# Fill matmuls at the start, Q casts straight from PSUM and a new instruction order in a chunk-select attention + ELU MLP kernel

## The chip, the cores and the metric

The kernel runs on one core of a Trainium2 chip. The metric is the device time of one execution in microseconds; the time before is 295.12 us, the median of three runs (294.37 to 295.87). The profiled execution has a span of 295.9 us.

A core has five engines with in-order queues of their own: TensorE (PE, matmuls and weight loads), VectorE (DVE), ScalarE (ACT), GpSimd (POOL) and SyncE (SP, which here only issues DMA transfers). Matmul results go to PSUM[...]; everything else is in SBUF.

## The reference, cut to what matters

Attention over 4 batches x 8 heads, 768 positions, head size 64. Per query, an upper bound of the score of each chunk of 32 keys selects the 6 best causal chunks; softmax attention runs over these. Then an MLP with 512 inputs, 2048 hidden units and ELU:

```python
k_min, k_max = k_chunks.min(axis=3), k_chunks.max(axis=3)        # per chunk of 32 keys
ub = sum(maximum(q * k_min, q * k_max), axis=-1)                 # per query and chunk
top_chunks = argsort(where(causal, ub, -1e9))[..., -6:]
scores = where(selected and causal, q @ k.T / 8, -1e9)
x = softmax(scores) @ v                                          # -> (3072, 512)
h = x @ w_in
out = where(h > 0, h, exp(minimum(h, 0)) - 1) @ w_out
```

## The kernel before, in words

The sequence of each batch is cut into blocks of queries: batch 0 into three of 256, the others into two of 384 (`CUTS`), nine blocks in all. Heads are taken in four pairs j, so a pair's K or Q is 128 partitions wide (two heads of 64).

For a block i, `load` brings K, Q and V in fp32, one DMA for each 128 positions. `prep_k(j, i)` transposes a pair's K on PE with the fp32 identity into a PSUM tile (L484), DVE takes maximum and minimum per chunk from it (L504) and forms their difference (L521), and ACT casts K to bf16: for the blocks in `DIRECT_K` (0 and 1) in one instruction per head straight from PSUM into `lhs` (L511), for others through `kb` and a DMA (L516, L519). `prep_q(j, i)` transposes Q in the same manner, ACT copies it to SBUF as `QTf` in fp32 (L534), and a bf16 cast per head goes into `rhs`: on ACT from `QTf` for the blocks in `QC_ACT` (0 and 1, L538), on POOL for the others (L542). DVE makes `Qrl`, the positive part (L545). The PSUM tile of K and Q is a `psM` bank for block 0 (`PSM_PREP`), of which there are four, and the single `psT` bank for every other block.

`select(i)` computes the bounds of all pairs with small fp32 matmuls (L563), DVE transposes them (L574), takes the eight largest per query (L581), compares (L585) and transposes the mask into rows 64 to 95 of `rhs` (L591 for blocks 0 to 2; for others L597 and a DMA `rhs<-msk`). `attend` computes scores (L625) with the mask as additional contraction rows, ACT takes the exponential (L641, L645), DVE multiplies the diagonal parts by a triangle (L652, L659), PE weighs V (L674), DVE divides (L683, L685), and the result is transposed into `xt` (by PE and DVE, L693 and L696, for the first and last block; by DMA, L698, for the others). `mlp` runs 16 hidden tiles (L713; ACT exponential L717, POOL minus one L719, DVE maximum and minimum L721) and then the output product (L732, ACT copy L736, store).

At the start DVE also initialises: `rhs` and `kst` and `selb` memsets (L774, L777, L779), the constant `econst` (L405) and the mask rows of four `lhs` tiles (L418).

The order is not written by hand. `Plan` takes every operation with an engine, a cost (`occ`), a latency (`lat`) and a priority, and lays them out in time: each engine takes the operation that can start first, and among those that can start at once the one with the lowest priority number. The operation list in this order is then emitted, so the plan fixes each engine's queue; on the chip each instruction still waits for its own semaphores. A priority is that of the stage (`span`) plus a number from `SHIFTS` for the stage, the engine and the block. `CAPS` is how many buffers of a kind exist.

Before each PE operation planned before `FILL_END` (70 us), the emission loop puts fill matmuls on a junk tile (L849) into planned holes, and a run of them ahead of the first real PE operation, whose number comes from that operation's planned start:

```python
for _ in range(int((o.start - pe - 100) / FILL_NS) if pe else int((o.start - FILL_FROM) / 90)):
    nc.tensor.matmul(o_bank[:, 400:512], lhsT=junk, rhs=junk[:, 0:112], start=True, stop=True)
```

The POOL queue issues the weights and some K, Q and V loads in the fixed order `SW_ORDER`, the first of them after a gate operation that reads the first K tile.

## Time and profile before

| | before |
|---|---|
| time, median of 3 | 295.12 us |
| span of the profiled execution | 295.9 us |
| PE busy | 277.3 us (94%), 2544 matmuls, 100 of them fills |
| DVE busy | 204.8 us (69%) |
| ACT busy | 196.4 us (66%) |
| POOL busy | 137.0 us (46%) |
| mean granted TensorE clock | 0.965 |
| DMA | 36.23 MB, mean 122 GB/s |

In a row of the profile, L-numbers are lines of the kernel; `out<-in` gives the tiles with their numbers left out; a bracket `[0.61 <-PE psM L484]` is the engine's idle time before the instruction and what ended it. PE's busy time covers matmuls from start to a modelled end, overlapping ones once, so a PE that is always busy need not be at its best rate. The clock is given as a share of full speed. A DMA share of 1.0 or more means that the core's 16 DMA engines have work all the time.

### The profile page before, as it was taken

How to read it: one execution, taken by the hardware profiler on the slowest of the kernel's cores; microseconds unless marked ns; L12 is line 12 of the kernel's file. 1: busy time of each engine (PE TensorE's matmuls, PEld its weight loads, DVE VectorE, ACT ScalarE, POOL GpSimd, SP SyncE). 2: the span in 40 equal slices, each digit the busy share in tenths (PEclk: the TensorE clock that was granted, in tenths of full speed). 3: DMA queues.
4: the chain of work that ended last, by engine and by line, in shares of the span. 5: the costliest groups of instructions: out<-in, count | busy, mean ns of one | idle time of the engine just before them, and what ended most of it. 6: DMA issues, size and time to landing. Idle time of an engine off the chain costs nothing.

```text
span 295.9 us, 7293 instructions
## 1 busy us (share of the span) xinstructions
PE 277.3 (94%) x2544; PEld 179.4 (61%) x2544; DVE 204.8 (69%) x667; ACT 196.4 (66%) x458; POOL 137.0 (46%) x278
## 2 busy tenths in 40 slices
PE   8576879999999998999999999999999999999993
PEld 8354557569658655666565556766565456655541
DVE  8778698897768886855699966666678727634620
ACT  2795587299559528997397349995496389854621
POOL 7697674034915924845365414750285024404510
PEclk9865798999999999999999999999999999999999
DMA  8889998268936665968845662602210420010001
GB/s 189 221 149 214 273 198 149 65 174 180 208 66 180 150 135 122 243 158 205 199 95 153 144 175 68 153 16 85 74 44 17 82 94 2 0 39 35 38 35 72
DMA packets 86885, 36.23 MB, mean 122 GB/s; under 512 B 74176, under 2 KB 82880, under 8 KB 86848
## 3 DMA queue, kind: packets, MB, share of 16 engines
q1 hardware_dynamic: 79424, 27.38, 37.7%
q0 software_dynamic: 5344, 7.87, 13.0%
q10 hardware_dynamic: 2080, 0.52, 0.8%
q8 instruction: 20, 0.33, 0.5%
q14 instruction: 17, 0.14, 0.2%
HBM read 27.26 MB, written 6.29 MB: 113 GB/s over the span
## 4 chain that ended last, share of the span: by engine, by line
PE 73%; DVE 13%; ACT 6%; DMA 4%; issue 2%; POOL 1%; SPq 0%; POOLq 0%; DVEq 0%; ACTq 0%
PE psM L713 23%; PE psM L732 23%; PE psS L625 10%; PE o_bank L674 6%; PE psT L484 5%; DVE gT L721 3%; PE psT L563 2%; DMA rhs<-msk 2%; PE o_bank L849 2%; ACT rhs L538 2%; DVE rhs L591 2%; DVE kmx L504 2%; ACT lhs L511 1%; DMA kld<-in_k_dram 1%; DVE thr L581 1%
## 5 line engine op out<-in xcount | busy, mean ns | idle before, releaser
L719 POOL TENSOR_SCALAR e<-e 128x384 f32<-128x384 f32 (+1 forms) x144 | 69.8, 489 | 120.6 <-ACT e L717 60.0
L713 PE MATMUL psM<-xt,w_in_sb 128*128 128x384 bf16 (+1 forms) x576 | 109.0, 313 | 1.6 <-DVE gT L721 1.4
L732 PE MATMUL psM<-w_out_sb,gT 128*128 128x512 bf16 x384 | 99.1, 379 | 0.0
L641 ACT ACTIVATE pt<-psS 128x384 bf16<-128x384 f32 (+1 forms) x164 | 87.7, 568 | 13.2 <-PE psS L625 12.7
L721 DVE SCALAR_TENSOR_TENSOR gT<-psM,e 128x384 bf16<-128x384 f32 (+1 forms) x144 | 71.8, 506 | 25.4 <-POOL e L719 24.0
L717 ACT ACTIVATE e<-psM 128x384 f32<-128x384 f32 (+1 forms) x144 | 68.8, 486 | 21.9 <-PE psM L713 18.4
L713 PEld LDWEIGHTS <-w_in_sb 128*128 128x128 bf16 x576 | 55.4, 99 | 28.1 <-issue 2.4
L625 PE MATMUL psS<-rhs,lhs 96*128 96x384 bf16 (+2 forms) x304 | 66.3, 286 | 2.5 <-DMA rhs<-msk 1.5
L732 PEld LDWEIGHTS <-gT 128*128 128x128 bf16 x384 | 36.0, 98 | 31.5 <-issue 1.2
L625 PEld LDWEIGHTS <-lhs 96*128 96x128 bf16 x312 | 29.4, 100 | 19.4 <-issue 2.3
L542 POOL TENSOR_SCALAR rhs<-QTf 64x384 bf16<-64x384 f32 (+1 forms) x56 | 29.4, 526 | 14.4 <-ACT QTf L534 10.8
L736 ACT ACTIVATE osb<-psM 128x512 f32<-128x512 f32 x24 | 14.4, 600 | 30.5 <-PE psM L732 30.3
L674 PEld LDWEIGHTS <-pt 128*128 128x128 bf16 x672 | 27.8, 99 | 9.8 <-issue 1.7
L674 PE MATMUL o_bank<-vext,pt 128*128 128x65 bf16 x672 | 30.9, 195 | 0.8 <-DVE on L685 0.5
L652 DVE TENSOR_TENSOR pt<-pt,tri 128x512 bf16<-128x512 bf16 x36 | 17.0, 475 | 7.0 <-ACT pt L641 6.6
L516 ACT ACTIVATE kb<-psT 128x384 bf16<-128x384 f32 (+1 forms) x28 | 13.7, 489 | 12.0 <-DVE kst L504 7.8
L504 DVE TENSOR_REDUCE kmx<-psT 128x12 f32<-128x384 f32 (+1 forms) x32 | 16.6, 519 | 6.7 <-PE psT L484 6.3
L534 ACT ACTIVATE QTf<-psT 128x384 f32<-128x384 f32 (+1 forms) x32 | 15.9, 498 | 7.6 <-PE psT L484 7.6
L475 POOL TENSOR_SCALAR vext<-vld 128x384 bf16<-128x384 f32 (+1 forms) x36 | 17.5, 509 | 5.7 <-DMA vld<-in_v_dram 3.0
L685 DVE TENSOR_TENSOR on<-o_bank,rcp 128x384 bf16<-128x384 f32 (+1 forms) x36 | 18.2, 506 | 0.6
L484 PE MATMUL psT<-ident_f,kld 128*128 128x128 f32 x88 | 16.0, 285 | 1.3 <-ACT QTf L534 0.6
L484 PE MATMUL psT<-ident_f,qld 128*128 128x128 f32 x88 | 15.8, 285 | 1.4 <-ACT lhs L511 1.0
(69 smaller groups left out, 241.6 us busy)
## 6 DMA issues: line engine op xcount, KB each, us to landing
out_dram<-osb SPq DMA_DIRECT2D x24, 256.0 KB, 2.2
kld<-in_k_dram SPq DMA_DIRECT2D x19, 256.0 KB, 4.0
qld<-in_q_dram SPq DMA_DIRECT2D x19, 256.0 KB, 3.9
vld<-in_v_dram SPq DMA_DIRECT2D x18, 256.0 KB, 3.5
lhs<-kb SPq DMA_DIRECT2D x48, 48.0 KB, 2.6
w_in_sb<-in_moe_w_in_dram POOLq DMA_DIRECT2D x4, 512.0 KB, 9.5
w_out_sb<-in_moe_w_out_dram POOLq DMA_DIRECT2D x4, 512.0 KB, 11.9
vld<-in_v_dram POOLq DMA_DIRECT2D x6, 256.0 KB, 5.0
```

Of the source, the lines that this page charges most:

```text
L484: nc.tensor.transpose(ps.get()[:, P * n:P * (n + 1)], xb.get()[:, n, hs, :].rearrange("p h d -> p (h d)"), ident_f)
L504: nc.vector.tensor_reduce(out=out, in_=psk.get()[:, 0:w].rearrange("p (c w) -> p c w", w=CHUNK), axis=AX.X, op=o)
L542: pool_op(110 + pool_ns(w), lambda h=h: nc.gpsimd.tensor_scalar(out=rhs[RH[i]][0:64, h, j, 0:w], in0=qtf.get()[64 * h:64 * h + 64, 0:w], s ...
L625: nc.tensor.matmul(sps.get()[:, o + pc:o + pc + n], lhsT=lhs[s][0:96, hd, P * kb:P * (kb + 1)], rhs=rhs[y][0:96, hd, j, c0 - lo:c0 - lo + ...
L641: op("ACT", act_ns(wtot), 140, lambda pt=pt, sps=sps, hd=hd, wtot=wtot: nc.scalar.activation(out=pt.get()[:, hd, 0:wtot], in_=sps.get()[:, ...
L674: nc.tensor.matmul(o3.get()[:, hd, qi, :], lhsT=pt.get()[:, hd, P * qt + off:P * qt + off + P], rhs=vexts[s][:, kb, hd, :], start=(kb == 0 ...
L685: op("DVE", dve_ns(w), 140, lambda: nc.vector.tensor_tensor(out=on.get()[:, 0:nt, :, :].rearrange("p q h d -> p h q d"), in0=o3.get()[:, : ...
L713: op("PE", 1 + w / 2.4, 200, lambda fc=fc, kk=kk, h_ps=h_ps: nc.tensor.matmul(h_ps.get()[:, 0:w], lhsT=w_in_sb[:, kk, P * fc:P * (fc + 1)] ...
L717: op("ACT", act_ns(w), 200, lambda e=e, h_ps=h_ps: nc.scalar.activation(out=e.get()[:, 0:w], in_=h_ps.get()[:, 0:w], func=AF.Exp), reads=[ ...
L719: op("POOL", pool_ns(w), 72, lambda e=e: nc.gpsimd.tensor_scalar(out=e.get()[:, 0:w], in0=e.get()[:, 0:w], scalar1=-1.0, scalar2=1.0, op0= ...
L721: g_ops.append(op("DVE", dve_ns(w), 130, lambda e=e, h_ps=h_ps, fc=fc: nc.vector.scalar_tensor_tensor(out=gT[fc // 4].get()[:, fc % 4, 0:w ...
L732: op("PE", 216, 200, lambda tt=tt, fc=fc, o_ps=o_ps: nc.tensor.matmul(o_ps.get(), lhsT=gT[fc // 4].get()[:, fc % 4, P * tt:P * (tt + 1)], ...
```

## The change

It has four parts.

1. The run of fill matmuls ahead of the first real PE operation is a fixed 30 (`FILL_FIRST`) in place of a number worked out from the plan. It was 79 in the kernel before.
2. For blocks 0 and 1 the two Q casts per pair read the PSUM tile itself and no longer the fp32 copy `QTf`; `QTf` is still made, for the bounds.
3. The planner assumes shorter latencies for what happens in the first 30 us (`EARLY`): 800 instead of 1500 ns after a DMA's last byte, and a margin of 20 instead of 80 ns after an engine operation. The cost of issuing a DMA from SP is taken as 20 to 30 ns more. Where an operation needs two buffers of one kind, it now waits until two are free.
4. All `SHIFTS` are new, found by a search over orders with that planner, so the order of all queues may differ.

The rest (spaces, an unused `VC_ACT`, a DVE form of the Q cast that no block uses) changes nothing that is emitted. The core of the diff:

```diff
-QC_ACT = (0, 1)
-VC_ACT = ()
+QC = {0: "ACT", 1: "ACT"}
...
+EARLY = 30e3
 FILL_NS = 500
-FILL_FROM = 1500
+FILL_FIRST = 30
 FILL_END = 70e3
 SHIFTS = {
...
-    ('init', 'DVE'): (2.32119, 0.0, 0.0, 4.74909, 8.35134, 25.74829, 26.2034, 24.17884, 8.09583),
+    ('init', 'DVE'): (0.44568, 0.0, 0.0, 7.20875, 0.34149, 0.36288, -7.77657, 2.31749, 2.55692),
...
-    ('prep_k', 'ACT'): (-19.18919, -30.78931, -27.5262, -6.91647, -6.7488, -6.36581, -3.55271, -15.77301, -8.33444),
-    ('prep_k', 'DVE'): (-28.28537, -41.41256, -18.41797, -26.42048, 4.76573, -40.62348, -18.36229, -14.34176, -9.12351),
+    ('prep_k', 'ACT'): (1.95557, 3.69513, -7.38461, -10.46153, -0.26086, -4.37445, -1.8812, -6.64019, -13.4638),
+    ('prep_k', 'DVE'): (13.79969, 29.17587, 8.56117, 5.61227, 22.14159, 14.74266, 22.42925, 17.17039, 5.0524),
...
-    ('prep_q', 'ACT'): (-33.9716, -32.60888, -11.98557, -31.52365, -6.14348, -38.53006, -19.34522, -0.18424, -32.21482),
+    ('prep_q', 'ACT'): (-7.71405, -9.34431, -9.87241, -11.61367, -10.7821, -10.84415, -1.41335, -1.46186, -6.15349),
...
-    ('score', 'ACT'): (-15.06279, 15.94173, -8.66685, 9.77749, -9.24225, 2.15661, -0.32595, 11.29037, -1.82453),
+    ('score', 'ACT'): (8.71172, 10.04522, 4.64753, 3.02921, -4.28376, 5.74632, 0.24677, -9.22653, 3.34877),
...
+                    need = {}
                     for x in o.bufs:
                         if x not in held:
-                            t = max(t, min(slots[x.cls], default=1e18))
+                            k = need[x.cls] = need.get(x.cls, 0) + 1
+                            t = max(t, sorted(slots[x.cls])[k - 1] if len(slots[x.cls]) >= k else 1e18)
...
-                done.end = clock + DMA_END
+                done.end = clock + (800 if clock < EARLY else DMA_END)
...
-                o.end = t + o.occ + o.lat + MARGIN
+                o.end = t + o.occ + o.lat + (20 if t < EARLY else MARGIN)
...
         for h in range(2):
-            if i in QC_ACT:
-                op("ACT", 150 + act_ns(w), 60, lambda h=h: nc.scalar.activation(
-                    out=rhs[RH[i]][0:64, h, j, 0:w], in_=qtf.get()[64 * h:64 * h + 64, 0:w], func=AF.Copy),
-                    reads=[qtf], writes=[r_q[RH[i]][j]])
+            how, r_out = QC.get(i, "POOL"), [r_q[RH[i]][j]]
+            if how == "ACT":
+                op("ACT", 60 + act_ns(w), 90, lambda h=h: nc.scalar.activation(
+                    out=rhs[RH[i]][0:64, h, j, 0:w], in_=psq.get()[64 * h:64 * h + 64, 0:w], func=AF.Copy),
+                    reads=[psq], writes=r_out)
                 continue
...
-                    for _ in range(int((o.start - pe - 100) / FILL_NS) if pe else int((o.start - FILL_FROM) / 90)):
+                    for _ in range(int((o.start - pe - 100) / FILL_NS) if pe else FILL_FIRST):
```

## The prediction

> **What bounds the kernel now.** I read four views in this order: the slices of the page, the busy time by stage, the chain at its end for the price of a matmul, and the timeline of the first 25 us. The slices come first because they show where TensorE (PE) is short of work and of clock.
>
> ```profile
> PE   8576879999999998999999999999999999999993
> PEclk9865798999999999999999999999999999999999
> DMA  8889998268936665968845662602210420010001
> ```
>
> A slice is 7.4 us. From the eighth slice on PE is full and at full clock; before that it has holes, the clock falls to 0.5, and the transfers are the busiest thing. The same by stage (span, then busy us and instructions of PE, weight loads, DVE, ACT, POOL; clock; DMA share; GB/s):
>
> ```profile
> 0.00:7.30 7.30, 6.20 (x78) 6.21 (x79) 5.98 (x15) 1.49 (x2) 5.12 (x23) 1.00 0.81 189
> 7.30:60.00 52.70, 42.54 (x412) 29.45 (x410) 42.09 (x165) 34.85 (x92) 31.07 (x56) 0.81 0.90 181
> 60.00:200.00 140.00, 137.16 (x1319) 91.24 (x1318) 105.50 (x337) 103.94 (x246) 71.95 (x144) 1.00 0.61 148
> 200.00:281.00 81.00, 80.99 (x697) 47.99 (x695) 49.69 (x150) 53.80 (x116) 27.81 (x54) 1.00 0.16 47
> 281.00:295.90 14.90, 10.42 (x49) 4.51 (x46) 1.59 (x3) 2.28 (x4) 1.02 (x2) 1.00 0.14 53
> ```
>
> Busy PE is not useful PE: the 78 matmuls of the first stage are fills. So I price the useful work by its dense spacing. The chain's end gives two prices, 4.55/28 = 162.5 ns for a 384-column matmul and 10.37/48 = 216 ns for a 512-column one:
>
> ```profile
> 276.51 4.55 PE psM L713 x28
> 281.06 10.37 PE psM L732 x48
> ```
>
> From other dense runs of the trace: 256 columns of L713 109 ns, L674 30 ns, an fp32 transpose (L484) 108.5 ns, scores (L625) 58, 112 and 165 ns for 128, 256 and 384 columns, a select group (L563) 0.4, 0.81, 1.03 or 1.45 us for 64, 192, 256 or 384 queries. The sum: L713 384 x 162.5 + 192 x 109 = 83.3 us; L732 384 x 216 = 82.9; L625 37.4; L674 672 x 30 = 20.2; L484 192 x 108.5 = 20.8; L563 9.2; L693 1.1; in all 255 us. By start times 30.0 of it lie before 60 us, 134.3 in 60 to 200, 80.5 in 200 to 281, 10.1 after. So PE time lost is 30.0, 5.7, 0.5 and 4.8 us. PE is the bound, and a change that leaves its work alone can gain only from the first 30 us of loss (7.3 before any real matmul, 22.7 from there to 60) and from the 5.7.
>
> The start, from the timeline and the transfer list:
>
> ```profile
> 1.10 6.44 PE L849 MATMUL o_bank<-junk 128*128 128x112 bf16 x79 [1.10 <-DVE junk L767]
> 4.26 2.93 DVE L418 COPY lhs<-econst 32x1536 bf16<-32x1536 bf16 x4
> 7.37 1.05 PE L484 MATMUL psM<-ident_f,kld 128*128 128x128 f32 x8
> 7.81 0.76 DVE L504 TENSOR_REDUCE kmx<-psM 128x8 f32<-128x256 f32 x2 [0.61 <-PE psM L484]
> 8.99 1.37 ACT L511 ACTIVATE lhs<-psM 64x256 bf16<-64x256 f32 x4 [6.68 <-DVE kst L504]
> kld<-in_k_dram ACTq DMA_DIRECT2D x1, 256.0 KB, 4.1
> ```
>
> The second half of block 0's K, issued at 0.98, landed 4.1 us later, at 5.1 (the SP half at 4.6). The transposes started at 7.37, right behind the fills: 2.3 us of an in-order queue stood between data and work. But DVE, whose reductions come next, was itself busy with L418 until 7.19; only 0.61 us of it was a wait for PE.
>
> **What the Trainium skill says.** "TensorE: Matmul & The Clock Gate", Part 1, has a cold clock of half rate that a window of some 3.4 us of activity releases. The trace agrees: fills start 93 ns apart and go to 49 ns near 6.2 us, and the clock falls to 0.5 at 13.0 us when work thins. (The stage view's 1.00 before 6.2 us is only the lack of a clock record there.) The same page (architectural detail) says ACT and DVE queues are strict FIFO; here four casts (L538, 11.40 to 13.09) stood ahead of QTf of the next pairs. "Perfetto Trace Analysis", Optimizing Scalar/DVE Operations, gives a ScalarE access overhead of about 93 ns on SBUF and 51 on PSUM. The trace has a 64x256 copy at 416 ns from SBUF (L538) and about 375 from PSUM (L511): 41 ns apart, in agreement. "PSUM — Partial Sum Buffer", on bank collisions, asks that a bank be guarded against any second engine; here PE waits on ACT's casts before it refills a bank (1.6 and 1.4 us in 7.3 to 60).
>
> ```profile
> PE psM L484 <- ACT lhs L511: 1.6, 1, 1.6
> PE psT L484 <- ACT lhs L511: 1.4, 2, 1.0
> ```
>
> **Part 1, the fill run.** 30 fills at 93 ns are 2.8 us, from 1.1 to 3.9, so the transposes start when K is there: about 5.2 instead of 7.37, 2.1 us earlier. How much is passed on? The new priority numbers put the reductions of block 0 (prep_k on DVE, from -28.3 to +13.8) behind all DVE initialisations (lhs copies 0.34, 0.36, -7.8 and 2.3; memsets 7.2 and 2.6), which end at 7.19. So the reductions move by the 0.61 us wait and no more; if they were let in ahead it could be 2.1. I take 0.6. Fewer fills also mean that the clock is probably cold from 6 to 13 us. A cold pair of transposes took 0.69 us (16.33) and a warm one 0.38 (35.61). Those of K hide behind L418; one pair of Q lies on the path: 0.3 us lost (0 to 0.6).
>
> **Part 2, the Q casts.** 16 casts (8 pairs, 2 heads) at 375 instead of 416 ns save 16 x 41 = 0.66 us of ACT. ACT is busy 5.27 of 5.40 us in 11 to 16.4 and 5.46 of 5.60 in 16.4 to 22, so it is the bound there and I count it in full: 0.65. The price is the bank. Today it is free after QTf (about 0.36 us); now also after two casts, 0.75 us more. Block 0 has four psM banks and K is ahead of Q in them anyway, so I take nothing there. Block 1 has the one psT bank:
>
> ```profile
> 17.09 0.38 ACT L534 ACTIVATE QTf<-psT 128x256 f32<-128x256 f32 x1
> 17.79 0.34 PEld L484 LDWEIGHTS psT<-ident_f,qld 128*128 128x128 f32 x2
> 17.89 0.84 ACT L538 ACTIVATE rhs<-QTf 64x256 bf16<-64x256 f32 x2
> 22.08 0.44 PE L484 MATMUL psT<-ident_f,kld 128*128 128x128 f32 x2 [0.56 <-ACT QTf L534]
> ```
>
> PE can load the next pair while ACT casts the last. Afterwards it can't: a cycle is PE 0.44 to 0.69, hand-overs 0.35, ACT 0.36 + 0.75, about 2.0 us, so four take 8.0 against 5.75 (16.33 to 22.08). That is 2.2 us more of the bank, ahead of which nothing waits but block 1's K transposes and its select (32.28). ACT can put the exponentials of block 0 into those holes.
>
> **Part 3, the order.** It moves every engine's queue; no work is added. Three idle stretches show what a better early order has to take: block 1's first K pair holds psT from 11.88 to 16.3, 4.4 us, since its casts come late on ACT, against 2.5 us that its steps need (PE 0.4, two reductions 0.8, two casts 0.75, hand-overs); QTf of pairs 2 and 3 of block 0 waits 1.7 us behind casts; and three K pairs of block 1 are left to 22 to 31, where ACT is busy 0.76 of 2.70 us (25.5 to 28.2). The first alone is 1.9 us of the one bank that leads to block 1's select. I take 2 us (0 to 4), which also has to pay for part 2's longer hold out of ACT's idle time after 25 us. From 60 us on I take 0: PE's recorded waits are 2.8 us in five places (1.5 for masks by DMA), which a new order may cure or make anew, -2 to +2. The other cost and latency numbers change only how the list is ordered, not an instruction.
>
> Sum: 0.6 - 0.3 + 0.65 + 2 = 2.95 us, so 295.1 - 2.9 = 292.2 us.
>
> **The rivals.**
> *No change (0.22).* Transfers run at 1.2 of 16 engines in 22 to 28 us and the last w_out block, issued at 36.9, landed 12.9 us later at 49.8, just when PE becomes full. If data sets that moment, an earlier start only waits longer. Against it: no PE wait in 7.3 to 60 is put down to a DMA. Time: 295.
> *Slower (0.19).* psT becomes the bound: 2.2 us later select for block 1, less 0.6 + 0.65 - 0.3 from the start, +1.25; and the new order brings one more mask wait like the longest of today (0.97). 295.1 + 2.2 = 297.3. For it: psT is held almost without a gap from 11.9 to 32.3. Against it: ACT stands idle after 25 us.
> *Larger (0.18).* The order recovers 3 us before 60 and 2 of the 5.7 after: 295.1 - 0.95 - 5 = 289.2.
>
> **How the numbers follow.** Main case 0.41. Faster by 0.5% is under 293.6: nearly all of the main and the larger case, a little of the first rival, 0.60; within 0.5% 0.21; slower 0.19. The range goes from 288.6, half a microsecond past the larger case, to 297.2, which leaves most of the slower case's upper half outside.
>
> **What would show it.** Step 1: first L484 near 5.2, first L504 near 7.2, a cold clock before 13 us. Step 2: casts from psM and psT near 375 ns, and QTf of block 1 some 2 us apart. Step 3: select of block 1 before 31 us, the loss to 60 us near 27 instead of 30, the loss in 60 to 200 still near 5.7. I am wrong if the reductions of block 0 come well before 7.2 (then more is gained), if block 1's select moves past 32.3, or if the loss after 60 us moves by more than 2.

## The result, and the profile after

| | before | after |
|---|---|---|
| time, median of 4 runs | 294.89 us (294.37 to 295.87) | 299.73 us (298.71 to 300.26) |
| after / before | | 1.0156, 95% interval 1.0115 to 1.0197 |
| time of the profiled run | 297.83 us | 299.32 us |

The change makes the kernel slower by 1.56%; the medians are 4.8 us apart. (A ratio here leaves out the few runs that were over 1.5% above the fastest of their kernel.) The prediction was 292.2 us, with 288.6 to 297.2 as its range. The sign was wrong and the range missed.

The two profiled runs are only 1.5 us apart, since that of before came out 2.9 us above its median. So the profiles show where time goes, and the amounts of a few tenths of a per cent rest on the medians. A third profile helps: the kernel before with only the fill run shortened (b_fill30 below), 293.67 us. That is the fastest of its twelve runs, whose median is 295.19.

Line numbers moved by two or three: transposes are now L482 (were L484), reductions L502, K casts L509, `QTf` L532, Q casts L537, the bounds of `select` L566 (L563), MAX8 L584 (L581), mask rows L594 (L591), scores L628 (L625), exponentials L644, weighing L677 (L674), `on` L688 (L685), `xt` L701 (L698), w_in L716 (L713), `gT` L724, w_out L735 (L732), fills L852 (L849). The kernels below whose order is a list have the same numbers as after, but fills at L850.

The slices of after, in the form shown for before:

```profile
PE   7577979889899999999999999999999999999993
PEclk9999999979999999999999999999999999999999
DMA  8799995169642945679347944753101130010011
```

The ninth digit of the clock row is the new thing: a 7 at 59.5 to 67 us, where before had a 9. (The 9s of the first four slices say nothing, since this trace holds no clock record before 30.7 us. Pairs of transposes take 0.63 to 0.69 us there, as cold ones did before.) PE itself has an 8 in the eighth, ninth and eleventh slice.

The busy time by stage (span, then busy us and instructions of PE, weight loads, DVE, ACT, POOL; clock; DMA share; GB/s):

```profile
0.00:7.30 7.30, 5.46 (x41) 4.66 (x41) 6.00 (x18) 1.49 (x2) 6.34 (x23) 1.00 0.83 194
7.30:60.00 52.70, 41.22 (x389) 28.92 (x394) 40.78 (x160) 34.98 (x92) 30.38 (x56) 1.00 0.86 175
60.00:200.00 140.00, 136.10 (x1293) 91.35 (x1309) 109.15 (x344) 104.44 (x244) 65.09 (x132) 0.99 0.63 150
200.00:281.00 81.00, 80.52 (x687) 48.37 (x695) 48.11 (x144) 52.53 (x114) 33.32 (x64) 1.00 0.14 43
```

These stages are too long to show the place of the loss, and a busy PE is not a PE at its best rate. As in the prediction, I price the useful matmuls by their dense spacing and call the rest of the time lost. (Records of 29 w_out matmuls are missing from the trace of after; I count w_out by its weight loads, which are complete, in every kernel.) Time lost so far, in us:

| until | before | after | b_fill30 |
|---|---|---|---|
| 30 us | 22.9 | 22.2 | 22.7 |
| 50 us | 30.0 | 28.2 | 27.3 |
| 55 us | 29.8 | 28.3 | 27.5 |
| 65 us | 31.0 | 32.9 | 28.8 |
| 80 us | 31.3 | 34.0 | 29.0 |
| 200 us | 35.5 | 37.1 | 31.5 |
| 280 us | 36.2 | 37.8 | 31.9 |

After is 1.5 us ahead of before at 55 us and 1.9 behind at 65. In those ten microseconds it loses 4.65 us, against 1.27 and 1.33 in the two others. From 80 us on nothing is added that before does not lose too.

Differences of about a microsecond between single traces need care, because the clock differs between executions of one program. It is at 0.5 from 43.7 to 47.1 us in before, but not in b_fill30. It is at 0.5 from 43.0 to 46.5 in a_again, which is the same program as after, but not in after; a_again has lost 29.1 us at 50 us, 0.9 more than after. The 3.3 us by which after loses more than the two others from 55 to 65 us are well beyond that.

This is the hole, on PE in after (start, duration, instruction; the bracket is the idle time before it and what ended it):

```profile
56.51 1.24 PE L735 MATMUL psM<-w_out_sb,gT 128*128 128x512 bf16 x5
58.91 0.21 PE L852 MATMUL o_bank<-junk 128*128 128x112 bf16 x1 [1.16 <-DVE on L688]
58.96 0.60 PE L628 MATMUL psS<-rhs,lhs 96*128 96x256 bf16 x4
...
60.03 0.33 PE L628 MATMUL psS<-rhs,lhs 96*128 96x256 bf16 x2 [0.42 <-ACT pt L644]
60.52 0.85 PE L628 MATMUL psS<-rhs,lhs 96*128 96x256 bf16 x4 [0.17 <-ACT pt L644]
61.66 0.96 PE L628 MATMUL psS<-rhs,lhs 96*128 96x256 bf16 x4 [0.29 <-ACT pt L644]
62.42 3.09 PE L716 MATMUL psM<-xt,w_in_sb 128*128 128x256 bf16 x16
```

Block 0's last w_out matmul ends at 57.75, block 1's first w_in matmul starts at 62.42. In the 4.67 us between them PE has 14 score matmuls of block 2 and two fills, about 1.5 us of work by their dense prices. What the first of them wait for, on DVE:

```profile
55.28 0.45 DVE L577 STREAM_TRANSPOSE ubT<-psT 128x256 f32<-128x256 f32 x1 [0.59 <-PE psM L566]
...
56.05 1.36 DVE L584 MAX8 thr<-ubT 128x8 f32<-128x17 f32 x16
...
57.97 0.44 DVE L594 STREAM_TRANSPOSE rhs<-selb 32x256 bf16<-32x256 bf16 x1
58.44 0.42 DVE L688 TENSOR_TENSOR on<-o_bank,rcp 128x256 bf16<-128x256 f32 x1
58.89 3.21 DVE L594 STREAM_TRANSPOSE rhs<-selb 32x256 bf16<-32x256 bf16 x7
```

The reader is to see three things. The scores need the masks, and the masks come out of a serial chain that `select(2)` (54.07 on PE) starts; the first mask ends at 58.41. (The bracket at 58.91 names `on`, because a fill, which writes the bank that `on` reads, stands ahead of the first score. It holds the queue for at most the last 0.5 us of that wait.) From 59.4 us on the waits on PE are put down to ACT's exponentials and no longer to masks: 0.42, 0.17 and 0.29 us in the brackets above. Exponentials end at 59.98, 60.46, 60.94, 61.60 and 62.09, and each time the next scores, which need one of the two `psS` banks (`CAPS`), start about 0.05 us later. And the work that could fill the hole, w_in of block 1, needs `on` of its last pair, which stands in DVE's queue behind those MAX8 rows. It runs at 58.44, its transfer lands at 61.20, and w_in, which stands behind seven score operations in PE's queue, starts at 62.42. The same place in b_fill30:

```profile
53.60 2.75 PE L732 MATMUL psM<-w_out_sb,gT 128*128 128x512 bf16 x12
...
56.52 0.60 PE L625 MATMUL psS<-rhs,lhs 96*128 96x256 bf16 x4
56.96 1.03 PE L732 MATMUL psM<-w_out_sb,gT 128*128 128x512 bf16 x4
57.83 0.65 PE L625 MATMUL psS<-rhs,lhs 96*128 96x256 bf16 x4
58.31 0.49 PE L713 MATMUL psM<-xt,w_in_sb 128*128 128x256 bf16 x3
```

There `select(2)` comes at 50.7, `on` of the last pair at 54.44, and w_in follows w_out after 0.32 us, with scores sprinkled between. By weight loads, 21 of block 0's 32 w_out matmuls still stand behind `select(2)` there, as in before; in after only 8 do.

The start, from the timeline of after and its transfer list:

```profile
1.06 2.98 PE L852 MATMUL o_bank<-junk 128*128 128x112 bf16 x30 [1.06 <-DVE warm L388]
2.69 2.36 DVE L420 COPY lhs<-econst 32x1536 bf16<-32x1536 bf16 x4
4.20 0.45 PE L482 MATMUL psM<-ident_f,kld 128*128 128x128 f32 x1 [0.16 <-POOL vext L426]
4.84 1.76 PE L482 MATMUL psM<-ident_f,kld 128*128 128x128 f32 x7 [0.20 <-DMA kld<-in_k_dram]
6.47 0.76 DVE L502 TENSOR_REDUCE kmx<-psM 128x8 f32<-128x256 f32 x2
```

Transposes start when K lands, and the reductions at 6.47, right when DVE ends its memsets. The transposes are 0.21 us apart here, where before had 0.11. Of the PSUM bank `psT` this is the stretch that matters, ACT's queue in after:

```profile
16.14 0.39 ACT L532 ACTIVATE QTf<-psT 128x256 f32<-128x256 f32 x1 [0.78 <-PE psT L482]
16.46 0.49 ACT L644 ACTIVATE pt<-psS 128x384 bf16<-128x384 f32 x1
16.85 0.36 ACT L537 ACTIVATE rhs<-psT 64x256 bf16<-64x256 f32 x1
17.12 0.48 ACT L644 ACTIVATE pt<-psS 128x384 bf16<-128x384 f32 x1
17.62 0.38 ACT L537 ACTIVATE rhs<-psT 64x256 bf16<-64x256 f32 x1
18.02 0.87 ACT L644 ACTIVATE pt<-psM 128x384 bf16<-128x384 f32 x2
19.00 0.38 ACT L532 ACTIVATE QTf<-psT 128x256 f32<-128x256 f32 x1
```

The order puts block 0's exponentials between `QTf` and the casts, so a Q pair takes 2.9 us of the bank, against 1.5 before. Further on, K pairs of block 1 follow each other 3.8 and 3.9 us apart (3.4 and 2.7 before), with evacuations of block 0's w_in stage between their steps, and block 2's first K pair stands ahead of `select(1)`:

```profile
33.84 0.40 PE L482 MATMUL psT<-ident_f,kld 128*128 128x128 f32 x2
...
36.69 0.44 PE L482 MATMUL psT<-ident_f,kld 128*128 128x128 f32 x2 [0.28 <-ACT lhs L509]
...
38.32 0.38 ACT L514 ACTIVATE kb<-psT 128x256 bf16<-128x256 f32 x1
...
38.75 0.40 PE L566 MATMUL psT<-QTf,kst 64*32 64x256 f32 x1 [0.65 <-ACT kb L514]
```

`select(1)` is at 38.75; it was at 32.3 before. In exchange block 0's MLP came earlier: its first w_in matmul at 26.5 instead of 28.6, its first w_out matmul at 42.7 instead of 48.3.

### The profile page after: what moved, and what is told of

The parts are those of the page before. It is cut to its first block, busy times and chain, and to the rows that moved or that the text cites. A ratio compares the mean times of both kernels' runs of the same rounds, so it can differ in the third digit from the quotient of the medians.

```text
span 297.6 us, 7176 instructions
## 1 busy us (share of the span) xinstructions
PE 275.4 (93%) x2466; PEld 178.9 (60%) x2495; DVE 206.3 (69%) x667; ACT 197.8 (66%) x458; POOL 137.2 (46%) x278
## 4 chain that ended last, share of the span: by engine, by line
PE 72%; DVE 13%; ACT 4%; POOL 3%; DMA 3%; issue 3%; SPq 0%; ACTq 0%; POOLq 0%
PE psM L735 23%; PE psM L716 23%; PE psS L628 10%; PE o_bank L677 6%; PE psT L482 5%; DVE gT L724 2%; PE psT L566 2%; POOL e L722 2%; DMA kld<-in_k_dram 2%; DVE on L688 1%; ACT pt L644 1%; DMA xt<-on 1%; DVE rhs L594 1%; DVE kmx L502 1%; DVE pt L655 1%
## 5 line engine op out<-in xcount | busy, mean ns | idle before, releaser
L716 PE MATMUL psM<-xt,w_in_sb 128*128 128x384 bf16 (+1 forms) x576 | 110.1, 315 | 0.6 <-DVE gT L724 0.3
L735 PE MATMUL psM<-w_out_sb,gT 128*128 128x512 bf16 x355 | 96.4, 379 | 1.3 <-issue 0.5
L724 DVE SCALAR_TENSOR_TENSOR gT<-psM,e 128x384 bf16<-128x384 f32 (+1 forms) x144 | 72.0, 507 | 31.2 <-POOL e L722 30.2
L644 ACT ACTIVATE pt<-psS 128x384 bf16<-128x384 f32 (+1 forms) x164 | 84.7, 551 | 11.7 <-PE psS L628 10.9
L720 ACT ACTIVATE e<-psM 128x384 f32<-128x384 f32 (+1 forms) x144 | 67.1, 473 | 32.7 <-PE psM L716 31.3
L716 PEld LDWEIGHTS <-w_in_sb 128*128 128x128 bf16 x576 | 56.2, 100 | 30.2 <-issue 1.9
L628 PE MATMUL psS<-rhs,lhs 96*128 96x384 bf16 (+2 forms) x304 | 65.3, 286 | 1.9 <-ACT pt L644 0.9
L735 PEld LDWEIGHTS <-gT 128*128 128x128 bf16 x384 | 36.2, 97 | 30.0 <-issue 2.0
L628 PEld LDWEIGHTS <-lhs 96*128 96x128 bf16 x312 | 29.8, 100 | 20.0 <-issue 3.4
L677 PEld LDWEIGHTS <-pt 128*128 128x128 bf16 x672 | 28.4, 99 | 8.8 <-issue 2.5
L677 PE MATMUL o_bank<-vext,pt 128*128 128x65 bf16 x672 | 31.4, 195 | 1.7 <-DVE on L688 1.5
L532 ACT ACTIVATE QTf<-psT 128x384 f32<-128x384 f32 (+1 forms) x32 | 15.3, 477 | 13.3 <-PE psT L482 11.9
L502 DVE TENSOR_REDUCE kmx<-psT 128x12 f32<-128x384 f32 (+1 forms) x32 | 16.6, 519 | 8.9 <-PE psT L482 8.5
L548 DVE TENSOR_SCALAR Qrl<-QTf 128x192 f32<-128x192 f32 (+3 forms) x36 | 13.9, 385 | 11.9 <-ACT QTf L532 11.4
L688 DVE TENSOR_TENSOR on<-o_bank,rcp 128x384 bf16<-128x384 f32 (+1 forms) x36 | 18.3, 507 | 0.6
L482 PE MATMUL psT<-ident_f,qld 128*128 128x128 f32 x88 | 16.2, 290 | 2.1 <-ACT QTf L532 1.0
```

The costliest lines, as they stand in the source:

```text
L482: nc.tensor.transpose(ps.get()[:, P * n:P * (n + 1)], xb.get()[:, n, hs, :].rearrange("p h d -> p (h d)"), ident_f)
L628: nc.tensor.matmul(sps.get()[:, o + pc:o + pc + n], lhsT=lhs[s][0:96, hd, P * kb:P * (kb + 1)], rhs=rhs[y][0:96, hd, j, c0 - lo:c0 - lo + ...
L644: op("ACT", act_ns(wtot), 140, lambda pt=pt, sps=sps, hd=hd, wtot=wtot: nc.scalar.activation(out=pt.get()[:, hd, 0:wtot], in_=sps.get()[:, ...
L677: nc.tensor.matmul(o3.get()[:, hd, qi, :], lhsT=pt.get()[:, hd, P * qt + off:P * qt + off + P], rhs=vexts[s][:, kb, hd, :], start=(kb == 0 ...
L688: op("DVE", dve_ns(w), 140, lambda: nc.vector.tensor_tensor(out=on.get()[:, 0:nt, :, :].rearrange("p q h d -> p h q d"), in0=o3.get()[:, : ...
L716: op("PE", 1 + w / 2.4, 200, lambda fc=fc, kk=kk, h_ps=h_ps: nc.tensor.matmul(h_ps.get()[:, 0:w], lhsT=w_in_sb[:, kk, P * fc:P * (fc + 1)] ...
```

## The experiments

"Ratio" is to runs of the kernel before on the same chip in the same rounds. In most of the kernels the order stands as a list (`ORDER`, numbers of the planner's operations) in place of the planner's run, so that single operations can be moved; a TensorE list is given by stage, with the block in brackets and counts of operations. Dates and losses are from one trace for each kernel.

| run | us | ratio | select(1) | select(2) | w_out end to w_in start, us | lost 55 to 65 | lost 45 to 70 |
|---|---|---|---|---|---|---|---|
| before (profiled run 297.8) | 294.89 | 1 | 32.3 | 53.0 | 0.32 | 1.27 | 2.25 |
| b_fill30 | 295.19 | 0.9991 | 31.1 | 50.7 | 0.32 | 1.33 | 1.71 |
| b30_red | 295.89 | 0.9993 | 31.7 | 52.7 | 0.32 | 1.16 | 2.05 |
| b30_psum | 297.65 | 1.0038 | 32.8 | 52.4 | 0.32 | 1.04 | 1.61 |
| h2_cut70 | 296.92 | 1.0019 | 31.7 | 52.6 | 0.32 | 1.16 | 2.05 |
| h2_sel2c | 296.95 | 1.0023 | 31.7 | 51.8 | 1.90 | 2.46 | 3.28 |
| h2_sel2b | 297.22 | 1.0042 | 31.9 | 51.2 | 3.46 | 3.55 | 4.70 |
| h2_sel2 | 299.41 | 1.0116 | 31.7 | 50.6 | 4.56 | 4.54 | 5.78 |
| h2_early_old | 299.68 | 1.0107 | 31.6 | 54.3 | 4.67 | 4.76 | 5.19 |
| h1_early_new | 297.85 | 1.0057 | 38.9 | 55.2 | 0.32 | 0.56 | 5.64 |
| a_qtf | 298.48 | 1.0071 | 38.9 | 54.2 | 4.66 | 4.76 | 5.69 |
| a_wi | 299.26 | 1.0107 | 38.0 | 54.2 | 3.00 | 3.33 | 3.83 |
| after | 299.73 | 1.0156 | 38.8 | 54.1 | 4.67 | 4.65 | 5.47 |
| a_again | 299.90 | 1.0117 | 38.6 | 54.9 | 4.56 | 4.10 | 6.01 |
| a_fill79 | 300.24 | 1.0169 | 38.8 | 55.0 | 4.69 | 4.19 | 6.27 |
| b30_late | 300.13 | 1.0156 | 31.7 | 55.9 | 0.54 | 5.77 | 7.01 |
| a_k2late | 301.21 | 1.0205 | 37.2 | 57.4 | 4.56 | 3.16 | 5.65 |

### The fill run

b_fill30 is the kernel before with the short run, and a_fill79 the kernel after with the long one.

```diff
-                    for _ in range(int((o.start - pe - 100) / FILL_NS) if pe else int((o.start - FILL_FROM) / 90)):
+                    for _ in range(int((o.start - pe - 100) / FILL_NS) if pe else 30):
```

```diff
-FILL_FIRST = 30
+FILL_FIRST = 79
```

> The kernel before with 30 instead of 79 fill matmuls at the start; every other instruction and every queue's order stay. Theory O (the new order lost the time: TensorE runs dry at 55 to 65 us because of what stands in the VectorE queue): the fills are not the cause, 293.5 to 295.5 us, with the first real transposes near 5 us and the reductions of block 0 near 7.2. Theory C (fewer fills leave TensorE at half clock for the first 30 us, and that lost the time): 297 to 300 us, and in the trace a pair of transposes at 0.69 us up to about 30 us. Theory P (the longer hold of the one psT bank by the casts lost the time): as O.

> The changed kernel with 79 fills at the start instead of 30; all else the same. Theory O: 299 to 302 us, since K's transposes wait for the fills again (up to 2 us more) and the order stays. Theory C: 295 to 297 us, near the kernel before. Theory P: 299 to 302 us.

Measured: 0.9991 (0.9967 to 1.0014) and 1.0169 (1.0129 to 1.0209, where after has 1.0156). Neither direction makes a difference that can be told. In b_fill30 the reductions start at 7.22, 0.6 us earlier as predicted, but `select(0)` only 0.1 us earlier (13.30). Its `select(1)` comes 1.2 us earlier (31.1), and still the end hardly moves. The fills are not the cause of the loss, and no gain from them can be told either.

b30_red goes further in the same place: b_fill30 with the four `econst` copies of DVE behind the first reductions, and the `QTf` of pairs 2 and 3 of block 0 ahead of two casts.

```diff
 DVE:
-init(4) init(7) init(5) init(6) ... prep_k(0)
+prep_k(0) ... init(4) init(5) ... init(6) init(7)
 ACT:
-cast cast QTf QTf
+QTf QTf cast cast
```

> The kernel before with 30 fills; on VectorE the reductions of block 0's K stand before the four lhs copies, two of which follow behind them and two behind the first two Qrl; on ScalarE QTf of pairs 2 and 3 of block 0 stand behind the casts of pair 0 instead of behind those of pairs 0 and 1. Theory of the prediction (VectorE's initialisation passes on only 0.6 of the 2.1 us that 30 fills set free): reductions near 5.6 instead of 7.2, select of block 0 near 12 instead of 13.3, and 294 to 294.8 us, 0.5 to 1 us under 30 fills alone. Theory S without more: what is won before 30 us counts only as far as block 2's select comes earlier than 50.7; if it doesn't, 295.2 us.

Measured: 0.9993 (0.9968 to 1.0018), as b_fill30. `select(0)` comes 0.4 us earlier (12.9), `select(1)` does not (31.7 against 31.1). No gain from the first 13 us can be told at the end.

### The casts from PSUM

a_qtf is the change with its own queues, but the casts read `QTf` in SBUF as before. b30_psum is b_fill30 with the casts reading PSUM, each pair's right behind its `QTf`. a_again is the change itself, its order written as a list.

```diff
-                    out=rhs[RH[i]][0:64, h, j, 0:w], in_=psq.get()[64 * h:64 * h + 64, 0:w], func=AF.Copy),
-                    reads=[psq], writes=r_out)
+                    out=rhs[RH[i]][0:64, h, j, 0:w], in_=qtf.get()[64 * h:64 * h + 64, 0:w], func=AF.Copy),
+                    reads=[psq, qtf], writes=r_out)
```

```diff
 ACT, b_fill30 to b30_psum (block 1, pair j):
-QTf  score  cast(QTf)  cast(QTf)
+QTf  cast(psT)  cast(psT)  score
```

(`psq` stays among the reads that the plan sees, so that the queues of a_qtf are those of the change. The instruction itself no longer reads it.)

```diff
-    plan.run()
...
-        for o in plan.order:
+        for n in ORDER:
+            o = plan.ops[n]
```

> The changed kernel with the same queues, but the Q casts of blocks 0 and 1 read the fp32 copy in SBUF again, so that a PSUM bank is free after the copy. Theory O: 299 to 301 us (0.66 us more ScalarE, some of it hidden). Theory C: the same. Theory P: 295.5 to 297.5 us, with the select of block 1 (L566) about 2 us earlier than in the changed kernel.

> The kernel before with 30 fills and the Q casts of blocks 0 and 1 reading PSUM, put directly behind the copy to QTf on ScalarE; all else in the old order. Theory P (holding the psT bank over the casts costs by itself): select of block 1 at 33 to 34 instead of 31.1 us and 296.5 to 298 us. If only the new order costs: select near 31 and 294 to 295.5 us, the 0.66 us of ScalarE gained or hidden.

> The changed kernel itself once more, its order written out as a list instead of planned, as the measure for the others of this call: 299 to 300.5 us by every theory.

Measured: in the old order the casts from PSUM cost 1.0038 / 0.9991 = 1.0047, about 1.4 us. The two intervals (1.0009 to 1.0067, 0.9967 to 1.0014) overlap a little, and they come from different rounds; against before in its own rounds 1.0038 is clear of 1. In the new order 1.0156 / 1.0071 and 1.0117 / 1.0071 give 1.0084 and 1.0046, again from different rounds: the two numerators are the same program. In the rounds of a_qtf itself a_fill79 stands at 1.0169, 1.0097 over a_qtf with intervals that lie apart, and 49 fills made no difference that could be told. So this part of the change costs half a per cent or more in the new order, and about half a per cent in the old one with less certainty. What the order alone costs is a_qtf against b_fill30, which share fills and casts and were run in the same rounds: 1.0071 / 0.9991 = 1.0080, 2.4 us, with intervals that lie apart.

In the old order the mechanism can be read on ACT. This is b30_psum:

```profile
18.80 0.38 ACT L532 ACTIVATE QTf<-psT 128x256 f32<-128x256 f32 x1 [0.98 <-PE psT L482]
19.08 0.76 ACT L537 ACTIVATE rhs<-psT 64x256 bf16<-64x256 f32 x2
20.67 0.38 ACT L532 ACTIVATE QTf<-psT 128x256 f32<-128x256 f32 x1 [0.32 <-PE psT L482]
...
22.55 0.38 ACT L532 ACTIVATE QTf<-psT 128x256 f32<-128x256 f32 x1 [0.32 <-PE psT L482]
```

A cycle is 1.88 us, where b_fill30 has 1.51. From the first `QTf` of block 1 to the next K cast it is 16.26 to 25.32, 9.06 us against 7.21. `select(1)` at 32.8 is 1.7 us later than in b_fill30, and at least 0.9 later than in the seven other kernels here with 30 fills, the old early order and casts from SBUF (31.6 to 31.9). How this reaches the end is not shown: `select(2)` at 52.4 is later than in b_fill30 (50.7) but not later than in b30_red and h2_cut70 (52.7 and 52.6), in whose traces the clock falls at 43 us. ACT is busy only 2.14 of the 6 us from 25 to 31 and does not win it back. In the new order the same cast changes no such date: a_qtf has `QTf` at 16.20, 19.02, 22.00, 24.48 and `select(1)` at 38.9, as after. There the pace comes from what the queues put between the pairs, scores on PE and exponentials on ACT. The traces of after and a_qtf have lost nearly the same up to 280 us, 37.8 and 37.4. Where the half per cent arises in that order stays open.

### Which half of the order

h1_early_new has the new order for what the kernel before plans into its first 50 us, and the old order later. h2_early_old is the reverse. Both have 30 fills and casts from SBUF.

```diff
 ORDER:
-all operations in the order of one plan
+operations of the first 50 us in the order of one plan, the rest in that of the other
```

> The operations that the planner of the kernel before starts in its first 50 us stand in the order of the changed kernel, all later ones in the order of the kernel before; Q casts read the SBUF copy, 30 fills. Theory E (the early order lost the time: select of block 1 at 38.8 instead of 31 us because of the chain through the one psT bank, then TensorE runs dry at 57 to 62 us): about as the changed order with SBUF casts, 297.5 to 299 us, select of block 1 near 38.8. Theory L (the later order lost it): 294.5 to 296 us.

> The reverse: the operations that the planner of the changed kernel starts in its first 50 us stand in the order of the kernel before, all later ones in that of the changed kernel; Q casts read the SBUF copy, 30 fills. Theory E: 294.5 to 296 us, select of block 1 near 31. Theory L: 297.5 to 299 us.

Measured: 1.0057 (1.0033 to 1.0081) and 1.0107 (1.0068 to 1.0145). Each half alone brings a loss of about the size of the whole, so they don't add, and neither expectation, that one half alone is to blame, came true. In h1_early_new `select(1)` is at 38.9, and the hole is at 45 to 55 us (4.4 us lost there). It is block 1's own chain that runs short of work there: PE waits 1.26 us for a mask before its scores at 46.45, while 21 w_out matmuls of block 0 stand further back, behind `select(2)`. h2_early_old has `select(1)` back at 31.6, but `select(2)` still at 54.3, since 17 w_out matmuls of block 0 stand ahead of it on PE:

```profile
50.17 3.19 PE L735 MATMUL psM<-w_out_sb,gT 128*128 128x512 bf16 x14
53.20 0.49 PE L628 MATMUL psS<-rhs,lhs 96*128 96x256 bf16 x4
53.53 0.81 PE L735 MATMUL psM<-w_out_sb,gT 128*128 128x512 bf16 x3
```

DVE had nothing to do from 51.0 to 54.5 us. So the question became whether it is the use of this spare work ahead of the chain, and the lack of it later, that costs the time.

### Spare work ahead of the chain or behind it

b30_late does to the old order what the new one does, in a larger dose: 17 w_out matmuls of block 0 go ahead of `select(2)`, nothing else. That leaves 4 behind it, where after and h2_early_old have 8.

```diff
 TensorE:
-weigh(1)x4  w_out(0)x4  select(2)  weigh(1)x4  w_out(0)x5  K(3)  w_out(0)x12  K(3)  score(2)x2
+weigh(1)x4  w_out(0)x21  select(2)  weigh(1)x4  K(3)x2  score(2)x2
```

> The mirror of that: the kernel before with 30 fills, and 17 matmuls of block 0's output product that stood behind block 2's select (L563) moved in front of it; nothing else moves. Theory S: select near 54 instead of 50.7 us, a hole of TensorE after it, 298 to 300 us instead of 295.2. If the place of the select doesn't matter: 295 to 296 us.

Measured: 1.0156 (1.008 to 1.0231), as large a loss as that of the whole change, from one move. On PE:

```profile
51.28 4.70 PE L735 MATMUL psM<-w_out_sb,gT 128*128 128x512 bf16 x21
...
56.93 0.60 PE L677 MATMUL o_bank<-vext,pt 128*128 128x65 bf16 x14
...
61.20 0.90 PE L482 MATMUL psT<-ident_f,kld 128*128 128x128 f32 x3 [3.03 <-ACT kb L514]
```

`select(2)` falls to 55.9, and DVE, idle for 4.7 us before, gets its bounds at 57.1. PE has nothing from 58.2 to 61.2, and the clock is at 0.5 from 59.9 to 66.7. The hole is of another make than that of after: the next K transposes wait for the `psT` bank, whose reductions stand behind the MAX8 rows in DVE's queue and end at 60.5. The first mask ends at 61.6, so the scores could not have filled the gap either.

The way back, in three steps from h2_early_old. h2_sel2 moves the 17 matmuls directly behind `select(2)`; h2_sel2b moves them also behind the weighing of block 1's last pair; h2_sel2c in addition lets the first 16 w_in matmuls in between the scores.

```diff
 TensorE, h2_early_old to h2_sel2:
-weigh(1)x4  w_out(0)x14  score(1)x2  w_out(0)x3  select(2)  w_out(0)x1   weigh(1)x4
+weigh(1)x4               score(1)x2              select(2)  w_out(0)x18  weigh(1)x4
 h2_sel2 to h2_sel2b:
-select(2)  w_out(0)x18  weigh(1)x4  w_out(0)x1
+select(2)  w_out(0)x1   weigh(1)x4  w_out(0)x18
 h2_sel2b to h2_sel2c:
-score(2)x7  w_in(1)x16
+score(2)x4  w_in(1)x4  score(2)  w_in(1)x4  score(2)  w_in(1)x4  score(2)  w_in(1)x4
```

> As h2_early_old, but the 17 matmuls of block 0's output product (L735) that stood before the select of block 2 (L566) in TensorE's queue now stand directly behind it; nothing else moves. Theory S (the time goes where block 2's select comes late: TensorE's spare work is spent before it and nothing is left to do while VectorE and ScalarE work through that select): select at 51 instead of 54.3 us, loss between 55 and 65 us under 2 us instead of 4.8, and 295 to 296.5 us instead of 299.7. If the new late order costs in other places (masks by DMA, later blocks): 298 to 300 us although the select is early.

> As h2_early_old, with the 17 w_out matmuls of block 0 placed behind select(2) and also behind the weigh of pair 3 of block 1, so that VectorE's rcp of that pair (L686), which stands ahead of the MAX8 rows in VectorE's queue, no longer waits for them. In h2_sel2 those 17 lay between select(2) at 50.6 and the weigh at 55.49, VectorE had nothing from 52.55 to 56.12 and the first scores of block 2 came at 59.1. Theory S (the loss is TensorE running out of prepared work while the chain select(2), MAX8, masks, scores of block 2 is late): select(2) stays near 50.6, the MAX8 rows begin near 52.5, the first scores of block 2 come near 55.5, the loss from 55 to 65 us falls from 4.6 to under 2.5, the time falls from 299.4 to 295 to 297. Rival O (something else in the later part of the new order costs the time, wherever the chain stands): the scores come early and the time still stays at 298.5 or above.

> As h2_sel2b, with one more move on TensorE's queue: the first 16 matmuls of block 1's w_in stage go from behind the tenth score of block 2 to between the earlier scores, four after the fourth and four after each of the next three. In h2_sel2b their input had been ordered at 56.3 us but they stood behind scores that wait for masks on VectorE, and began at 62.0. Theory S in its narrower form (TensorE lacks prepared work while it waits for masks): w_in begins near 59.5, the loss from 55 to 65 us falls from 3.6 to 2.5 or less, the time from 297.2 to 295 to 296.5. If the hole is set by the masks alone, loss and time stay as they were.

Measured: 1.0116 (1.005 to 1.0182), 1.0042 (1.0019 to 1.0066), 1.0023 (0.9999 to 1.0047). The first step missed: `select(2)` came to 50.6 as expected, but the loss stayed at 4.54. The trace of that run shows why. The weighing of the last pair now stood behind the 17 and ended near 56.1, and DVE's `rcp` that waits for it stands ahead of the MAX8 rows in DVE's queue, so DVE idled from 52.55 to 56.12. With that mended MAX8 begins at 53.17 and the time falls by 0.7% (from different rounds, and the intervals overlap). The scores themselves still start only at 58.42, since 24 w_out matmuls now stand ahead of them, so the loss fell to 3.55 and not to the 2.5 I expected. In h2_sel2b one also sees that masks alone don't make the hole. The last one ends at 59.22, and from then on PE waits for exponentials only:

```profile
58.42 0.60 PE L628 MATMUL psS<-rhs,lhs 96*128 96x256 bf16 x4
...
59.71 0.33 PE L628 MATMUL psS<-rhs,lhs 96*128 96x256 bf16 x2 [0.63 <-ACT pt L644]
60.20 0.85 PE L628 MATMUL psS<-rhs,lhs 96*128 96x256 bf16 x4 [0.17 <-ACT pt L644]
61.34 0.81 PE L628 MATMUL psS<-rhs,lhs 96*128 96x256 bf16 x4 [0.29 <-ACT pt L644]
```

The third step took the loss to 2.46, as expected; the time went from 297.22 to 296.95, in the expected direction but not to be told apart from none. On PE in h2_sel2c:

```profile
59.02 0.60 PE L628 MATMUL psS<-rhs,lhs 96*128 96x256 bf16 x4
...
60.80 0.39 PE L628 MATMUL psS<-rhs,lhs 96*128 96x256 bf16 x2 [0.17 <-ACT pt L644]
61.03 0.60 PE L716 MATMUL psM<-xt,w_in_sb 128*128 128x256 bf16 x4
61.47 0.38 PE L628 MATMUL psS<-rhs,lhs 96*128 96x256 bf16 x2
```

Between h2_early_old and h2_sel2c only places in TensorE's queue differ, and 0.8% of the time with them; these two intervals lie apart.

### The later part, and the change mended

h2_cut70 has the old order for all that the kernel before plans into its first 70 us and the new order from there. a_wi is the change with block 1's w_in made ready earlier. a_k2late is the change with block 2's first K pair moved behind `select(1)`.

```diff
 a_wi, DVE:
-rcp(1)  MAX8 rows  on(1)
+rcp(1)  on(1)  MAX8 rows
 a_wi, SP:
-lhs(2)x4  xt(1)x4
+xt(1)  lhs(2)x2  xt(1)  lhs(2)x2  xt(1)x2
 a_wi, TensorE:
-score(2)x7  w_in(1)x16
+score(2)x4  w_in(1)x4  score(2)  w_in(1)x4  score(2)  w_in(1)x4  score(2)  w_in(1)x4
 a_k2late, TensorE (and the reductions on DVE):
-K(2)  ...  select(1)
+...  select(1)  K(2)
```

> The old order for every instruction that the planner of the kernel before starts in the first 70 us, the changed kernel's order for all that follows; 30 fills, casts of the later blocks from SBUF. Theory S (the order costs what it costs between 45 and 65 us, while block 2's chain is late and TensorE has no prepared work): no hole at 57 to 62 us, the loss from 55 to 65 us is near 1.3 as in the old order, the time is 294.5 to 296 as for the old order with 30 fills (295.2). Rival O (the later part of the new order costs something wherever the chain stands): 297 or above, with the difference after 70 us.

> The changed kernel with block 1's w_in stage made ready earlier: VectorE's on of pair 3 directly behind its rcp instead of behind the MAX8 rows, two of the four transposes of xt ahead of the last four lhs loads on SyncE, and the first 16 w_in matmuls between the early scores of block 2. Theory S: w_in begins near 60 instead of 62.4, the loss from 55 to 65 us falls from 4.65 to about 3, and the time from 299.7 to about 298. Rival M (the masks set the stretch): no change, 299.5 to 300.5.

> The changed kernel with one thing moved: the transposes, casts and copies of block 2's first K pair, which stand ahead of block 1's select matmuls in it, are placed behind them. Theory D (the longer PSUM hold delays select(1), and what stands before it in the psT banks delays it further): select(1) comes 1.5 to 2.5 us earlier, near 36.7 instead of 38.8, and block 2's select no later than 54.1. If the early lateness is what is paid for at 57 to 62 us, the time falls by 1 to 2 us, to 298 to 299. If the filler spent ahead of select(2) decides, wherever select(1) stands, the time stays at 299.5 to 300.5.

Measured: h2_cut70 1.0019 (0.9992 to 1.0045). The stretch loses 1.16 us and w_in follows w_out after 0.32 us. Its median of 296.92 is above the 296 I expected, but the kernel before took 296.2 in those rounds; the later part of the new order costs 0.28% over b_fill30 with an interval that holds zero. From 70 to 280 us it loses 4.6 us, which lies within the 3.0 to 5.0 us of the four kernels with the old order (before, b_fill30, b30_red, b30_psum). So what can be seen of the order's cost arises before 70 us.

a_wi: the loss fell to 3.33 us with w_in from 60.9 (expected: about 3 and near 60), and the clock did not fall in the hole. The time, 299.26, is not the 298 I expected: 1.0107 (1.0041 to 1.0174), below after (1.0156) but not below a_again (1.0117): inconclusive as a time.

a_k2late: `select(1)` came 1.5 us earlier as expected (37.2), and the time was 1.0205 (1.0146 to 1.0264), no gain. For the K pair that had been moved held the bank until 41.7, then all steps of block 2 that use the one bank came later, and `select(2)` came at 57.4 instead of 54.1. So an earlier `select(1)` bought in this way gains nothing.

No version of these beats the kernel before: the best, b_fill30, is level with it.

## Why the prediction was wrong

**What bounds the kernel.** That PE's work sets the time and only its lost time can be won holds: the useful work is the same in all these kernels, and a large part of the differences between them is lost time of 45 to 70 us. The two don't go in step, with one trace for each kernel: h1_early_new loses 5.64 us there at a ratio of 1.0057, a_wi 3.83 at 1.0107.

**Part 1.** The transposes started at 4.20 and 4.84 (predicted 5.2) and the reductions at 6.47 (7.2), so more was won there than the 0.6 us I counted: 7.81 to 6.47 is 1.3 us. The fills alone bring the 0.6 (7.22 in b_fill30); the rest is DVE's own start, whose four copies take 2.36 us here and 2.93 before. The cold clock that I counted as 0.3 us is there as well, with transposes 0.21 us apart in after and b_fill30; what it cost was not separated. None of it made a measurable difference at the end (b_fill30 0.9991, b30_red 0.9993). A gain of 0.6 us, and any up to about 1 us, lies inside these intervals; the 2.2 us by which b30_red's reductions come earlier (5.60) does not.

**Part 2.** The price of a cast was right: 0.36 to 0.38 us, against 0.42 from SBUF. This agrees with the Trainium skill ("Perfetto Trace Analysis", Optimizing Scalar/DVE Operations), which has ScalarE's access to PSUM cheaper. The bank's price was also about right, 1.85 us over block 1's Q against the 2.2 predicted. What failed is the sentence that the order would pay for this "out of ACT's idle time after 25 us". ACT was idle there, and it did not help: the K pairs behind go through the same single bank, each with PE, two reductions and two casts in turn, and idle time of one of these engines does not shorten that chain. So in place of the 0.65 us counted as a gain, b30_psum measures a loss of about 1.4 us in the old order. In the new one, "ACT can put the exponentials of block 0 into those holes" is what happened, and it is no help: the scores and exponentials in between set a cycle of 2.5 to 3.0 us, with either cast (a_qtf).

**Part 3.** This is the step that failed most. I took 2 us of gain from a better early order, `select(1)` before 31 us and a loss to 60 us near 27. `select(1)` came at 38.8, the loss was 30.3, and the order costs 2.4 us (a_qtf against b_fill30). An early gain is not even certain: at 50 us after has lost 1.8 us less than before, but 0.9 more than b_fill30. The new order takes block 0's MLP first and block 1's and block 2's chain later. That MLP work is the main filler that PE has while block 2's masks and exponentials are made, and 8 of its 32 w_out matmuls were left behind `select(2)` instead of 21. I had looked for idle places before 60 us and asked how they could be filled; I had not asked with what, and what would be left. Of my three signs of being wrong the second came true (`select(1)` past 32.3). The first did too (reductions before 7.2), without the larger gain that it was to mean. The third did not (the loss from 60 to 200 us went from 5.5 to 6.8).

**The rivals.** The slower case had the right side and, for the bank, about the right size (1.25 us against 1.4 in the old order). Its path did not come true: it had the bank delay `select(1)` by 2.2 us, and in the new order `select(1)` is 6.5 us late with either cast (a_qtf 38.9), so it is the order that delays it. For the order it had one more mask wait of 0.97 us; what came instead was 2.4 us (0.8%). Hence 297.3 where 299.7 was measured, and a range that ended 2.5 us short. In after no wait of PE from 55 to 65 us is put down to a DMA.

What is shown: the order alone costs 0.8%; a single move of 17 w_out matmuls in the old order costs as much as the whole change (b30_late); undoing such a placement step by step, with w_in put between the scores, wins 0.8% (h2_early_old to h2_sel2c). That in the change itself the loss has this cause is supported by the same hole at the same place in h2_early_old (gap 4.67 us, loss 4.76), but the attempts at mending it there did not win the time back clearly (a_wi). Open is also where the casts cost their half per cent in the new order.

## What to carry to other kernels

When an order is changed early on, don't judge it by how much idle time it removes there. Look at which work it used to fill it, and check at the next serial chain (here select, MAX8, masks, scores, exponentials) that prepared work is left to run beside it, and that it stands between the waiting instructions in the queue and not behind them. Where several engines hand on a single buffer in turn, add up the hand-overs of the buffer and not the busy time of one engine: in b30_psum ACT's idle time did not pay for the longer hold. And a short early gain of the first 13 us has to be followed to a later date, such as the next select, before it is counted.

## What was not expected

- A hole with sparse work costs twice. The clock was at 0.5 from 61.4 to 64.8 us in after, 3.4 us, although PE was not idle in the hole. The Trainium skill ("TensorE: Matmul & The Clock Gate", Part 1) has the half rate set in after an idle window of some 3.4 us. Here the 3.4 us ahead of the fall held ten scores and two fills, about 1.1 us of scores by their dense prices, so a window that was only sparse was followed by the half rate. The 16 w_in matmuls at 62.42 took 3.09 us, 16 x 109 ns = 1.74 when warm, so by this estimate about 1.3 of the 4.65 us are the clock. The two kernels that put w_in between the scores did not show the fall at this place. The stretch from 60 to 65 us in after, then in h2_sel2c, where the last number but two is the clock:

```profile
60.00:65.00 5.00, 4.44 (x23) 2.80 (x23) 3.95 (x10) 3.96 (x9) 0.51 (x2) 0.66 0.83 200
```

```profile
60.00:65.00 5.00, 3.96 (x33) 3.07 (x33) 1.86 (x6) 4.86 (x13) 0.83 (x3) 1.00 0.81 204
```

- The gap between the last w_out and the first w_in matmul goes with the loss of 55 to 65 us: 0.32 us of gap with 1.0 to 1.3 lost, 1.90 with 2.46, 3.00 with 3.33, 3.46 with 3.55, 4.67 with 4.65. Where the hole lies elsewhere (h1_early_new, b30_late, a_k2late) it doesn't, and a_again and a_fill79, whose half clock runs on to 67 us, lose 4.1 and 4.2 with gaps of 4.6 and 4.7.
- Either half of the new order brings about the loss of the whole, 0.6% and 1.1% against 0.7% (a_qtf).
- 49 fill matmuls more or less at the start, some 3.2 us of an in-order queue, make no difference to the time in either order.
